# Weight gradients computed piece by piece inside attention forward, in a one-core backward kernel of a transformer block

## Chip, cores, metric

The kernel runs on one core of one Trainium2 chip. The metric is device microseconds (us) of one execution. Each time quoted is the median of the executions, with the lowest and highest. The times of the profile come from one profiled execution and lie within 0.3% of these.

## The reference

The kernel computes one transformer block (adaptive layer norm, attention, an MLP with a squared ReLU) and all gradients of it, in bf16, for 2048 tokens of width 512, 32 heads of 16, and an MLP width of 1792. Cut to what matters:

```python
def _fwd_reference(A_x, A_wqkv, A_wo, B_x, B_w1, B_b1, B_w2, B_b2, c, w_mod):
    mod = (silu(c) @ w_mod)                        # sa, ca, ga, sb, cb, gb
    h = layernorm(x) * (1 + ca) + sa
    x = x + ga * attention(h, A_wqkv, A_wo)        # softmax over 2048 keys, 32 heads
    h = layernorm(x) * (1 + cb) + sb
    x = x + gb * (relu(h @ B_w1 + B_b1) ** 2 @ B_w2 + B_b2)
    return x

def reference(...):
    out, vjp = jax.vjp(f, A_x, A_wqkv, A_wo, B_w1, B_b1, B_w2, B_b2, c, w_mod)
    return (out, *vjp(grad_out))                   # out_0, then nine gradients
```

Three of the nine gradients are in question here. They are sums over all 2048 tokens: out_3 (of `A_wo`, 512x512), out_4 (of `B_w1`, 512x1792) and out_6 (of `B_w2`, 1792x512).

## The kernel before

The five engines are called PE (TensorE), DVE (VectorE), ACT (ScalarE), POOL (GpSimd) and SP (SyncE, which only issues DMAs). P is 128, FC is 14 (1792 / 128), DC is 4 (512 / 128), QC is 4 (chunks of 512 queries).

Attention forward runs 512 "units". A unit is four heads, 512 queries and 128 keys: four matmuls for the scores, two exponentials of 128x1024 on ScalarE, four matmuls that multiply the values. When the 128 units of one query chunk are done, that chunk's "dense" work can start: output projection, layer norm, MLP forward, MLP backward, gradient of the attention output. It is a Python generator, and the loop takes one step of it per unit, so that its matmuls run while ScalarE takes exponentials. Chunks 0 to 2 are mixed in this way. Chunk 3 has nothing left to be mixed with and runs alone.

```python
with tc.manual_schedule(engines={PE.engine, ACT.engine}):
    for u in range(NF + 6):
        ...                              # fload, fscore(u): scores and exponentials
        if 2 <= u < NF + 2:
            fpv(u - 2)                   # exponentials times values
        if dense:
            if wait > 0:
                wait -= 1
            else:
                wait = next(dense[0], -1)     # one step of the dense chunk
                ...
```

The dense chunk, cut to the order of its parts and of its weight loads. `wA` and `wB` are one buffer each, so a load waits until the last reader of the former content is done:

```python
def dense_chunk(c, O_c, act):
    w1_nat = load_wA(False)
    w2_nat = load_wB(False)
    ...                                  # projection, layer norm, h2
    yield 10
    for fc in range(FC):                 # MLP forward with w1_nat
        ...
        yield 0
    w2T = load_wA(True)                  # four transposing DMAs
    yield 1
    for ti in range(4):                  # MLP output product with w2_nat: ~20 steps
        ...
    w1T = load_wB(True)
    for fc in range(FC):                 # MLP backward with w2T
        ...
    for ti in range(4):                  # gradient of h2 with w1T
        ...
    yield 8
    for ti in range(4):                  # gradient of the attention output, with woT
        ...
```

So before the change each weight load had other work in front of its first use: the transposed w2 had the whole output product.

After forward came a phase of its own for the three weight gradients. It loaded its operands again from DRAM, and built a padded transpose of `A_wqkv` (`wT_bld`) that the last phase needs:

```python
for key, src in (("gf", gf_st), ("O", o_st), ("da", da_st), ("h2", h2_st)):
    ...                                  # 2 MB each, back from DRAM
wT_bld = big.tile([P, 16, D], BF, name="wT_bld")
...                                      # 12 transposing loads, 96 small DMAs
for oc in range(DC):
    acc = psg.tile([P, 512], F32, name="aw", tag="aw")
    for t in range(TT):
        PE.matmul(acc[:], toks["O"][:, t, oc * P:(oc + 1) * P], toks["da"][:, t, :], ...)
    ...                                  # copy, DMA to out_3; then out_6 and out_4 alike
```

Attention backward follows (512 units of four heads, 128 queries and 512 keys, with four exponentials each; its transposes `dsT` are DMAs on the SP queue), and then a last phase.

Of the kernel before, what the change touches and what calls it, by code (L numbers as in the profile page):

```python
# [17 lines left out]
BF = dt.bfloat16  # L18
# [16 lines left out]
def kernel(  # L35
# [55 lines left out]
    da_st = dram.tile([P, TT, D], BF, name="da_st")  # L91
    h2_st = dram.tile([P, TT, D], BF, name="h2_st")
    gf_st = dram.tile([P, TT, D], BF, name="gf_st")
    q_st = dram.tile([P, TT, QPAD], BF, name="q_st")
    k_st = dram.tile([P, TT, QPAD], BF, name="k_st")
    stok_st = dram.tile([QC, P, 4 * FF], BF, name="stok_st")
    dztok_st = dram.tile([QC, P, 4 * FF], BF, name="dztok_st")
    wT_st = dram.tile([P, 16, D], BF, name="wT_st")
# [60 lines left out]
    for ic in range(DC):  # L159
        for t in range(3):  # L160
            src = wqkv_nat[:, ic, t * 512:(t + 1) * 512].rearrange("p (hg h d) -> p hg h d", hg=HG, h=4)
            dst = wpadT[:, ic, t].rearrange("p hg (h c) -> p hg h c", h=4)[:, :, :, 0:DH]
            POOL.tensor_copy(dst, src)

# [115 lines left out]
    with ExitStack() as ph:  # L280
# [43 lines left out]

        def dense_chunk(c, O_c, act):
            ts = slice(4 * c, 4 * c + 4)
            w1_nat = load_wA(False)
            w2_nat = load_wB(False)
# [6 lines left out]
            gf_c = cb.tile([P, 4, D], BF, name="gf_c", tag="hd")  # L335
            POOL.tensor_tensor(gf_c[:], g_c[:], gb_bc.unsqueeze(1).to_broadcast([P, 4, D]), ALU.mult)
            SP.dma_start(out=gf_st[:, ts, :], in_=gf_c[:])
# [33 lines left out]
            h2_c = cb.tile([P, 4, D], BF, name="h2_c", tag="hd")  # L371
            POOL.tensor_tensor(h2_c[:], xn2_c[:], cb1_bc.unsqueeze(1).to_broadcast([P, 4, D]), ALU.mult)
            POOL.tensor_tensor(h2_c[:], h2_c[:], sb_bc.unsqueeze(1).to_broadcast([P, 4, D]), ALU.add)
            SP.dma_start(out=h2_st[:, ts, :], in_=h2_c[:])
            yield 10
            rT = cb.tile([P, FC, 512], BF, name="rT", tag="rT")
            sT = cb.tile([P, FC, 512], BF, name="sT", tag="sT")

            def to_tokens(src, dst, f0, f1):
                tk = cb.tile([P, 16, P], BF, name="tk", tag="tk", bufs=2)  # L380
                SP.dma_start(out=tk[:, 0:4 * (f1 - f0), :], in_=flat(src[:, f0:f1, :]), transpose=True)
                SP.dma_start(out=dst[:, 512 * f0:512 * f1], in_=flat(tk[:, 0:4 * (f1 - f0), :]))

            for fc in range(FC):
# [9 lines left out]
                if fc % 4 == 3 or fc == FC - 1:  # L394
                    to_tokens(sT, stok_st[c], fc // 4 * 4, fc + 1)
# [3 lines left out]
            for ti in range(4):  # L399
                t = 4 * c + ti  # L400
                pf = mm()
                for fc in range(FC):
                    PE.matmul(pf[:], sT[:, fc, ti * P:(ti + 1) * P], w2_nat[:, fc, :], start=(fc == 0), stop=False)  # L403
                    if fc % 4 == 3:
                        yield 0
                PE.matmul(pf[:], ones_bf[0:1, 0:P], b2row[0:1, :], start=False, stop=True)
                gfprod = wk.tile([P, D], BF, name="gfprod", tag="ta")
                DVE.tensor_tensor(gfprod[:], pf[:], g_c[:, ti, :], ALU.mult)
                rowsum(0, gfprod[:], t)
                ftmp = wk.tile([P, D], BF, name="ftmp", tag="tb")  # L410
                DVE.tensor_tensor(ftmp[:], pf[:], gb_bc, ALU.mult)
                DVE.tensor_tensor(x1_c[:, ti, :], ftmp[:], x1_c[:, ti, :], ALU.add)
                yield 0
            SP.dma_start(out=out0_v[:, ts, :], in_=x1_c[:])
            w1T = load_wB(True)
            dzT = rT
            for fc in range(FC):
# [8 lines left out]
                if fc % 4 == 3 or fc == FC - 1:  # L426
                    to_tokens(dzT, dztok_st[c], fc // 4 * 4, fc + 1)
                yield 0
            yield 1
            dx1_c = cb.tile([P, 4, D], BF, name="dx1_c", tag="od")  # L430
            da_c = cb.tile([P, 4, D], BF, name="da_c", tag="hd")
            for ti in range(4):
                t = 4 * c + ti
                pdh = mm()
                for fc in range(FC):
                    PE.matmul(pdh[:], dzT[:, fc, ti * P:(ti + 1) * P], w1T[:, fc, :],
                              start=(fc == 0), stop=(fc == FC - 1))
                    if fc % 4 == 3:
                        yield 0
                xn2 = xn2_c[:, ti, :]  # L440
# [19 lines left out]
                DVE.tensor_tensor(da_c[:, ti, :], dx1_c[:, ti, :], ga_bc, ALU.mult)  # L460
                proda = wk.tile([P, D], BF, name="proda", tag="tc")
                DVE.tensor_tensor(proda[:], dx1_c[:, ti, :], a_c[:, ti, :], ALU.mult)
                rowsum(3, proda[:], t)
                yield 0
            SP.dma_start(out=dx1_st[:, ts, :], in_=dx1_c[:])
            daT = cb.tile([P, 4, DC, P], BF, name="daT", tag="T4")
            SP.dma_start(out=daT.rearrange("p t o q -> p (t o) q"), in_=flat(da_c), transpose=True)
            SP.dma_start(out=da_st[:, ts, :], in_=da_c[:])
            dOs_c = cb.tile([P, 4, D], BF, name="dOs_c", tag="od")
            dOp = flat(cb.tile([P, FC, 512], BF, name="dOp", tag="sT"))[:, 0:4 * HG * P]  # L470
            dOp = dOp.rearrange("p (t g c) -> p t g c", t=4, g=HG)
            POOL.memset(dOp, 0.0)
            yield 8
            for ti in range(4):
                t = 4 * c + ti
                pdo = mm()
                for oc in range(DC):
                    PE.matmul(pdo[:], daT[:, ti, oc, :], woT[:, oc, :], start=(oc == 0), stop=(oc == DC - 1))
                src = pdo.rearrange("q (g h d) -> q g h d", g=HG, h=4)
                dst = dOs_c[:, ti, :].rearrange("q (g h d) -> q g h d", g=HG, h=4)  # L480
                rb = r_inv[:, t, :].rearrange("q (g h) -> q g h", g=HG).unsqueeze(3).to_broadcast([P, HG, 4, DH])
                DVE.tensor_tensor(dst, src, rb, ALU.mult)
                POOL.tensor_copy(dOp[:, ti].rearrange("q g (h c) -> q g h c", h=4)[:, :, :, 0:DH], dst)
                prodo = wk.tile([P, D], BF, name="prodo", tag="tb")
                DVE.tensor_tensor(prodo[:], dOs_c[:, ti, :], O_c[:, ti, :], ALU.mult)
                delta = wk.tile([P, H], F32, name="delta", tag="delta")
                DVE.tensor_reduce(delta[:], prodo.rearrange("q (h d) -> q h d", d=DH), AX.X, ALU.add)
                auxdst = dOp[:, ti].rearrange("q g (h c) -> q (g h) c", h=4)[:, :, DH:DH + 1].rearrange("q h o -> q (h o)")
                DVE.tensor_scalar(auxdst, delta[:], -1.0, None, ALU.mult)
                if ti % 2 == 1:  # L490
                    dOT = cb.tile([P, 16, P], BF, name="dOT", tag="tk", bufs=2)
                    SP.dma_start(out=dOT[:], in_=dOp[:, ti - 1:ti + 1].rearrange("p t g c -> p (t g c)"), transpose=True)
                    q0 = c * 512 + (ti - 1) * P
                    for hg in range(HG):
                        SP.dma_start(out=dOtP[hg][:, q0:q0 + 2 * P].rearrange("p (t q) -> p t q", t=2),
                                     in_=dOT.rearrange("p (t g) q -> p g t q", t=2)[:, hg])
                yield 0
            SP.dma_start(out=dOs_st[:, ts, :], in_=dOs_c[:])
# [26 lines left out]
        def fpv(u):  # L525
# [13 lines left out]
            if kt == TT - 1:  # L539
                ostage = wk.tile([P, 512], F32, name="ostage", tag="ostage")  # L540
# [29 lines left out]
        with ExitStack() as ph2:  # L570
# [3 lines left out]
            with tc.manual_schedule(engines={PE.engine, ACT.engine}):  # L574
                for u in range(NF + 6):
# [6 lines left out]
                    if dense:  # L582
                        if wait > 0:
                            wait -= 1
                        else:
# [435 lines left out]
```

## Time and profile before

3380.86 us (3377.52 to 3382.63, four executions).

| stretch | from | to | us |
|---|---|---|---|
| preparation | 0 | 289 | 289 |
| attention forward, dense chunks 0 to 2 mixed in | 289 | 1279 | 990 |
| dense chunk 3 alone | 1279 | 1412 | 134 |
| weight-gradient phase | 1412 | 1617 | 205 |
| loads, then attention backward from its first exponential (1635) | 1617 | 3070 | 1453 |
| last phase | 3070 | 3386 | 316 |

The table of stretches of the kernel before comes first. Its columns are the stretch in us from the start, its length, the busy time of each engine with its number of instructions, the granted TensorE clock, the mean busy share of the DMA engines, and what they moved.

```profile
core 0: us, PE busy (x) PEld busy (x) DVE busy (x) ACT busy (x) POOL busy (x), PEclk, DMA share, GB/s
287.00:533.00 246.00, 225.56 (x1064) 42.26 (x1064) 5.54 (x8) 245.24 (x268) 8.98 (x9) 0.50 0.17 52
1040.00:1278.00 238.00, 207.21 (x1228) 56.21 (x1237) 89.52 (x172) 226.66 (x246) 47.09 (x45) 0.78 0.49 121
1278.00:1412.00 134.00, 73.03 (x271) 28.67 (x275) 78.22 (x159) 9.54 (x14) 39.24 (x38) 0.75 0.66 124
1412.00:1450.00 38.00, 1.18 (x3) 0.50 (x4) 1.28 (x2) 0.00 (x0) 6.93 (x1) 0.51 0.68 223
1450.00:1617.00 167.00, 114.63 (x536) 53.97 (x540) 10.32 (x17) 10.30 (x18) 1.20 (x1) 0.84 0.42 152
```

In forward ScalarE is full: 245.24 of 246 us with attention alone, 226.66 of 238 with a dense chunk mixed in. In the two weight-gradient rows ScalarE does almost nothing (0 and 10.30 us), and TensorE works for 116 of 205 us. So these 205 us are serial, and the change wants to put their matmuls under ScalarE's exponentials.

That there is room is shown by one unit of forward with a dense step, from the time line of TensorE of the kernel before (start, us, engine, line, operation, output and inputs, count):

```profile
648.18 1.02 PE L420 MATMUL pm<-gfT,wA 128*128 128x512 bf16 x4
649.13 0.39 PE L521 MATMUL psST<-qt_sb,kt_sb 32*128 32x512 bf16 x4
649.46 0.40 PE L537 MATMUL oacc<-ET,vaug 128*32 128x512 bf16 x4
```

A unit lasts 1.92 us for ScalarE, and TensorE needs 0.39 + 0.40 us for attention and 1.02 us for four dense matmuls of 128x512.

The group of the forward exponentials on the page of the kernel before says how much ScalarE waited: its busy time, the mean of one in ns, then its idle time just before these instructions and what ended most of it.

```profile
L523 ACT ACTIVATE ET<-psST 128x1024 bf16<-128x1024 f32 x1024 | 945.5, 1311 | 34.7 <-PE psST L521 34.5
```

### The profile page before, as it was taken

The numbers are of one execution on the slowest core, as the hardware profiler recorded it, in microseconds if no ns is written. First come the engines' busy times: TensorE is split into PE (matmuls) and PEld (weight loads), VectorE is DVE, ScalarE is ACT, GpSimd is POOL, SyncE is SP. The second block draws the span as 40 slices with busy tenths as digits, with TensorE's granted clock in tenths as the row PEclk, the third lists the DMA queues.
The fourth block names the chain that finished last, engine by engine and source line by source line (L and its number), as shares of the span: only waits on it lengthen the run. The fifth ranks groups of instructions, "written<-read, shape, count | busy, mean of one in ns | idle before, by whom it ended". The sixth has DMA issues, their size and how long they took to land.

```text
span 3386.2 us, 47396 instructions
## 1 busy us (share of the span) xinstructions
PE 2663.9 (79%) x17485; PEld 788.3 (23%) x17549; DVE 1932.1 (57%) x2770; ACT 2157.3 (64%) x3474; POOL 372.3 (11%) x345
## 2 busy tenths in 40 slices
PE   2778998888888885348697889898898978885746
PEld 1232111221221222114122222222222222222312
DVE  8852002332343344400587878788887878884772
ACT  0006999999999992000586878787787868784202
POOL 3000001121121132300110010101010101010000
PEclk7986555975975976778788878888878889897867
DMA  3124001661662654763999999999999999997113
GB/s 128 55 107 150 29 29 47 136 173 52 138 166 57 137 155 100 167 211 115 219 200 213 199 211 197 207 205 204 208 198 209 198 215 201 201 201 182 63 62 94
DMA packets 1388742, 511.31 MB, mean 151 GB/s; under 512 B 1321939, under 2 KB 1359575, under 8 KB 1386205
## 3 DMA queue, kind: packets, MB, share of 16 engines
q1 hardware_dynamic: 1368782, 502.51, 70.8%
q10 hardware_dynamic: 19728, 5.77, 0.8%
q8 instruction: 138, 2.26, 0.3%
q14 instruction: 94, 0.77, 0.1%
HBM read 112.29 MB, written 74.08 MB: 55 GB/s over the span
## 4 chain that ended last, share of the span: by engine, by line
PE 36%; DMA 21%; ACT 18%; DVE 12%; issue 6%; SPq 3%; ACTq 2%; POOL 0%; DVEq 0%; POOLq 0%
DMA dsT<-dS_u 16%; ACT ET L523 14%; PE psS_u L724 7%; PE dqacc L776 5%; ACT E_u L726 4%; PE accVK L761 3%; PE ppad L266 3%; PE accVK L752 2%; PE psST L521 2%; DVE dS_u L738 2%; PE psS_x L724 2%; PE pm L387 2%; ACTq L636 1%; PE pm L420 1%; PE pm L403 1%
## 5 line engine op out<-in xcount | busy, mean ns | idle before, releaser
L738 DVE TENSOR_TENSOR dS_u<-psD_u,E_u 128x1024 bf16<-128x1024 f32 x1024 | 1189.4, 1218 | 248.5 <-PE psD_u L736 166.5
L726 ACT ACTIVATE E_u<-psS_u 128x512 bf16<-128x512 f32 x1536 | 866.3, 633 | 307.2 <-PE psD_u L736 274.0
L523 ACT ACTIVATE ET<-psST 128x1024 bf16<-128x1024 f32 x1024 | 945.5, 1311 | 34.7 <-PE psST L521 34.5
L724 PE MATMUL psS_u<-ik,iq 32*128 32x512 bf16 x1536 | 517.2, 434 | 27.0 <-DVE KS_tok L677 19.1
L521 PE MATMUL psST<-qt_sb,kt_sb 32*128 32x512 bf16 x2048 | 464.6, 507 | 85.2 <-ACT ET L523 37.7
L736 PE MATMUL psD_u<-iv,ido 32*128 32x512 bf16 x2048 | 448.4, 432 | 18.9 <-DVE dS_u L738 11.4
L776 PE MATMUL dqacc<-dsT,KS_tok 128*32 128x512 bf16 x2048 | 212.7, 503 | 161.0 <-DMA dsT<-dS_u 149.2
L726 ACT ACTIVATE E_u<-psS_x 128x512 bf16<-128x512 f32 x512 | 333.9, 652 | 2.2 <-PE psD_u L736 1.7
L537 PE MATMUL oacc<-ET,vaug 128*32 128x512 bf16 x2048 | 270.4, 517 | 0.6 <-ACT ET L523 0.6
L541 DVE COPY ostage<-oacc 128x512 f32<-128x512 f32 x32 | 22.0, 688 | 373.6 <-PE oacc L537 373.6
L761 PE MATMUL accVK<-E_u,dOs_tok 128*16 128x512 bf16 x2048 | 226.3, 432 | 0.0
L724 PE MATMUL psS_x<-ik,iq 32*128 32x512 bf16 x512 | 210.6, 411 | 0.6
L521 PEld LDWEIGHTS <-kt_sb 32*128 32x128 bf16 x2048 | 91.4, 96 | 461.7 <-issue 456.8
L724 PEld LDWEIGHTS <-iq 32*128 32x128 bf16 x2048 | 99.1, 93 | 378.6 <-issue 378.0
L736 PEld LDWEIGHTS <-ido 32*128 32x128 bf16 x2048 | 124.8, 93 | 228.4 <-issue 203.7
L791 POOL TENSOR_TENSOR dQacc<-dQacc,dqtmp 128x512 f32<-128x512 f32 x64 | 81.1, 1268 | 843.0 <-ACT dqtmp L786 843.0
L641 ACT ACTIVATE wblk<-aw 128x512 bf16<-128x512 f32 x9 | 5.4, 597 | 229.4 <-PE aw L648 125.2
L752 PE MATMUL accVK<-dS_u,qz_12652 128*32 128x512 bf16 x1024 | 113.1, 430 | 6.8 <-ACT vkb L764 5.8
L752 PE MATMUL accVK<-dS_u,qz_12651 128*32 128x512 bf16 x1024 | 112.0, 427 | 7.0 <-ACT vkb L764 6.1
L266 PE MATMUL ppad<-xn1T,wpadT 128*128 128x512 bf16 x376 | 98.7, 408 | 21.8 <-DVE stagep L269 16.2
L850 ACT ACTIVATE dqkv_tok<-ptq 128x64 bf16<-128x64 bf16 x128 | 28.6, 224 | 119.8 <-PE ptq L844 119.8
L776 PEld LDWEIGHTS <-KS_tok 128*32 128x32 bf16 x2048 | 52.1, 105 | 221.2 <-issue 179.0
(1021 smaller groups left out, 2496.9 us busy)
## 6 DMA issues: line engine op xcount, KB each, us to landing
kt_sb<-KtP SPq DMA_DIRECT2D x32, 512.0 KB, 3.7
dsT<-dS_u SPq DMA_TRANSPOSE x512, 5.1
wA<-in_B_w_dram SPq DMA_DIRECT2D x4, 1792.0 KB, 8.8
wB<-in_B_w_dram SPq DMA_DIRECT2D x4, 1792.0 KB, 7.7
stok_st<-tk SPq DMA_DIRECT2D x12, 512.0 KB, 3.0
dztok_st<-tk SPq DMA_DIRECT2D x12, 512.0 KB, 4.0
QtP<-stagep SPq DMA_DIRECT2D x8, 512.0 KB, 2.8
KtP<-stagep SPq DMA_DIRECT2D x8, 512.0 KB, 2.9
```

The source lines that it names most:

```text
L266: PE.matmul(pp[:], wpadT[:, ic, which, hg, :], h1T[:, ic, qc * 512:(qc + 1) * 512], start=(ic == 0), stop=(ic == DC - 1))
L521: PE.matmul(ps[:, hi, :], kt_sb[r:r + 32, kt * P:(kt + 1) * P], qt_sb[r:r + 32, :], start=True, stop=True, tile_position=(r, 0))
L523: ACT.activation(ET[:, 2 * pair:2 * pair + 2, :], ps[:], AF.Exp, scale=SCALE)
L537: PE.matmul(oacc[32 * hq:32 * hq + 32, :], lhsT, ET[:, hq, :], start=(kt == 0), stop=(kt == TT - 1), tile_position=(0, 32 * hq), skip_grou ...
L724: PE.matmul(psS[:], st["q"][r:r + 32, qt * P:(qt + 1) * P], st["k"][r:r + 32, kc * 512:kc * 512 + 512], start=True, stop=True, tile_positi ...
L726: ACT.activation(bst[u][0][:, hq, :], psS[:], AF.Exp, scale=SCALE)
L736: PE.matmul(psD[:, hi, :], st["do"][r:r + 32, qt * P:(qt + 1) * P], st["v"][r:r + 32, kc * 512:kc * 512 + 512], start=True, stop=True, til ...
L738: DVE.tensor_tensor(dS_u[:, 2 * pair:2 * pair + 2, :], psD[:], E_u[:, 2 * pair:2 * pair + 2, :], ALU.mult)
L752: PE.matmul(cur["vk"][32 * hq:32 * hq + 32, :], hst[hg]["qz"][:, qt, hq, :], bst[u][1][:, hq, :], start=(qt == 0), stop=False, tile_positi ...
L761: PE.matmul(acc[32 * hq:32 * hq + DH, :], dOs_tok[:, qt, (hg * 4 + hq) * DH:(hg * 4 + hq + 1) * DH], E_u[:, hq, :], start=False, stop=(qt ...
L776: PE.matmul(acc[32 * hq:32 * hq + 32, :], KS_tok[:, kc * 4 + kt, h * DH:h * DH + 32], tT[:, :, hq * 4 + kt, :], start=(kt == 0), stop=(kt ...
L791: POOL.tensor_tensor(dst2, dst, tmp[:], ALU.add)
```

## The change

Intent: take the weight-gradient phase out. Each chunk computes its share of the three gradients at once, while its operands are still in SBUF, as 34 "pieces". A piece is four matmuls (128 tokens each, 512 columns, 256 in four of the pieces), a VectorE copy into one of three buffers `dwp`, and a DMA into a partial sum in DRAM: chunk 0 writes it, chunks 1 and 2 add to it in the DMA (`accum_op`), chunk 3 loads it, adds it to its own result and writes the output. At most one piece runs per unit, and only in units without a dense step. To have the operands of the pieces early, the MLP output product is placed behind the MLP backward. The padded transpose of `A_wqkv` is written row-wise during preparation and read by 16 transposing DMAs at the start of attention backward.

```diff
-    da_st = dram.tile([P, TT, D], BF, name="da_st")
-    ...                                  # h2_st, gf_st, stok_st, dztok_st, wT_st
+    dw_st = dram.tile([DC + FC + 16, P, 512], F32, name="dw_st")
+    wpad_st = dram.tile([D, 16 * P], BF, name="wpad_st")
 ...
+        def dw_piece(c, i, dst, ops, w):
+            if c == QC - 1:
+                part = wk.tile([P, 512], F32, name="dwp", tag="dwp", bufs=3)
+                SP.dma_start(out=part[:, 0:w], in_=dw_st[i][:, 0:w])
+            acc = mm()
+            for ti in range(4):
+                PE.matmul(acc[:, 0:w], ops[ti][0], ops[ti][1], start=(ti == 0), stop=(ti == 3))
+            if c == QC - 1:
+                res = wk.tile([P, 512], BF, name="dwr", tag="ta")
+                DVE.tensor_tensor(res[:, 0:w], acc[:, 0:w], part[:, 0:w], ALU.add)
+                SP.dma_start(out=dst, in_=res[:, 0:w])
+            else:
+                part = wk.tile([P, 512], F32, name="dwp", tag="dwp", bufs=3)
+                DVE.tensor_copy(part[:, 0:w], acc[:, 0:w])
+                if c == 0:
+                    POOL.dma_start(out=dw_st[i][:, 0:w], in_=part[:, 0:w])
+                else:
+                    POOL.dma_start(out=dw_st[i][:, 0:w], in_=part[:, 0:w], accum_op=ALU.add)
 ...
         def dense_chunk(c, O_c, act):
             w1_nat = load_wA(False)
-            w2_nat = load_wB(False)
+            w1T = load_wB(True)
 ...                                       # MLP forward; its pieces are queued by later(dw_piece, ...)
             w2T = load_wA(True)
             yield 1
-            for ti in range(4):           # MLP output product
-                ...
-            w1T = load_wB(True)
             ...                           # MLP backward with w2T, then gradient of h2 with w1T
+            def mlp_out():
+                w2_nat = load_wB(False)
+                yield 1
+                ...                       # the output product, as before
+            if act:                       # chunk 3
+                yield 0
+                yield from attn_grad()
+                yield from mlp_out()
+            else:
+                yield from mlp_out()
+                yield from attn_grad()
 ...                                       # in the loop over units:
+                    if pend and pend[0][0] <= u and not open_group[0] and not stepped:
+                        _, f, args = pend.pop(0)
+                        f(*args)
 ...
-    with ExitStack() as ph:               # the weight-gradient phase and wT_bld: removed
-        ...
 ...
         load_head(0)
+        for j in range(16):
+            SP.dma_start(out=wT_pad[:, j, :], in_=wpad_st[:, j * P:(j + 1) * P], transpose=True)
```

## The prediction

> **What bounds the kernel now.** One core, 3381.5 us. The table of stretches shows: preparation to 287 us; attention forward with dense chunks 0 to 2 mixed in, 287 to 1278; dense chunk 3 alone, to about 1412; the weight-gradient phase to 1617; attention backward to 3073; the rest to 3386. In attention forward ScalarE is the limit: 227 of 238 us busy in 1040:1278; a unit takes 1.92 us. TensorE has room: a timeline at 646 us shows a unit as 0.39 us of scores, 0.40 of PV and 1.02 of four dense matmuls, with ScalarE at 30.0 of 30.0 us in 616:646. The weight-gradient phase is serial: 115 us of TensorE in 1450:1617, before it about 40 us of reloads and building wT.
>
> **Removed.** The weight-gradient phase: -205 us, all on the chain of waits.
>
> **Added in attention forward.** 34 pieces per chunk: four matmuls, a 0.69 us VectorE copy, a GpSimd DMA adding 256 KB into DRAM. About 3 run in the dense chunk's waits; 31 run one per unit after its end. The matmuls cost what a dense step costs, so I expect them hidden under ScalarE, with the granted clock near 1.0 (the Trainium skill, "TensorE: Matmul & The Clock Gate", Part 1: activity releases the half clock; the trace agrees: 0.50 in 740:786 with attention only, 0.92 to 1.00 with dense steps). An accumulating DMA must come from GpSimd (the skill, "DMA: Bandwidth & Descriptors", SWDGE vs HWDGE vs iDMA); this trace has none. With three buffers it may take about 5 us before the engines wait. I allow +15 us, uncertain.
>
> **Moved: the product behind the backward.** Two weight loads lose their cover. Transposed w2 must land two units (3.9 us) after its buffer is free; its four transposes take 1.5 to 3.3 us each to issue and 5.5 us to land: about 15 us, so TensorE stalls 10 to 12 us and ScalarE about 10. Plain w2 (8 us to land): ScalarE about 3. Three chunks: +39 us. ScalarE gaps of about 4 us at 734, 985, 1235 may go: -9. Attention forward in sum: +45 us (+25 to +80).
>
> **Chunk 3 alone (134 us now)** gains 34 pieces, each with a partial-sum load, an add and an output DMA: 0.95 us TensorE, 0.7 VectorE, partly in gaps (7 us each for w2 and OT, 6 for daT). I expect 150 to 165 us: +22.
>
> **Start of backward.** About 20 us of loads stay. Sixteen transposed wT loads on the same queue ahead of dsT: +5. One 2 MB load less in the last phase: -5.
>
> **Sum.** 3381 - 205 + 45 + 22 = about 3245 us. Range 3190 to 3310. Faster by over 2%: 0.90; within 2%: 0.08; slower: 0.02.
>
> **What would show it.**
> - No serial weight-gradient stretch; backward's first exponential near 1500 us instead of 1635.
> - Attention forward 1015 to 1070 us instead of 991; per chunk one ScalarE gap of 8 to 12 us while TensorE waits for the DMA into wA, one of 2 to 5 for wB.
> - The 31-piece stretches: unit 1.9 to 2.2 us, clock near 1.0. A unit of 2.5 us, with VectorE copies waiting for the accumulate DMA, would mean that the DMA limits.
> - The chunk-3 stretch 150 to 165 us.
>
> **What would make it wrong.** An accumulating DMA of 8 us or more (a unit 0.8 us longer in 93 units: +75 us); chunk-3 pieces serialized behind one in-order DMA queue (+40); wT transposes holding up dsT (+20); or w2 loads hidden better than I think (-35).

## The result, and the profile after

The changed kernel took 3342.85 us (3337.01 to 3347.24, four executions) against 3380.86: a ratio of 0.9888 (95% interval 0.987 to 0.9905). A ratio is the mean time of one kernel's runs over that of the other's of the same rounds, so it isn't quite the ratio of the medians. The prediction was 3245 us with a range of 3190 to 3310; the measured time lies 33 us above that range.

To say where the time went, forward is cut by its units: the k-th pair of exponentials in the trace is unit k. A dense chunk occupies 92 units (135 to 227, 263 to 355, 391 to 483). The 32 units after it (for chunk 2 the 29 units to the end of forward) are called the late stretch here; there the 31 remaining pieces run, one per unit. "Chunk 3 and on" goes from forward's last exponential to backward's first.

| us in the trace | before | after | difference |
|---|---|---|---|
| preparation | 289.0 | 291.3 | +2 |
| three dense parts | 177.9 / 176.6 / 176.7 | 192.6 / 191.9 / 189.6 | +43 |
| three late stretches | 65.2 / 64.3 / 59.6 | 75.1 / 87.7 / 86.8 | +60 |
| chunk 3 and on (before: and the weight gradients) | 356.5 | 192.4 | -164 |
| backward, first to last exponential | 1434.8 | 1460.4 | +26 |
| last phase | 316.1 | 308.9 | -7 |
| span | 3386.2 | 3345.0 | -41 |

(The rest of forward, attention alone, changed by about 1 us. One late stretch is known only roughly: wt_in_j and tail_bufs, two of the runs below whose edits don't touch forward, have 94.9 and 97.3 us for chunk 1 where after has 87.7, and 1097.0 and 1098.3 us for the whole of forward where after has 1092.1.) Of the 205 us of the phase that went, four fifths came back elsewhere. The table of stretches of the kernel after, with the same columns:

```profile
core 0: us, PE busy (x) PEld busy (x) DVE busy (x) ACT busy (x) POOL busy (x), PEclk, DMA share, GB/s
289.50:541.00 251.50, 228.94 (x1084) 43.09 (x1077) 8.78 (x16) 249.04 (x272) 8.96 (x9) 0.50 0.18 49
1022.00:1090.00 68.00, 42.95 (x256) 12.98 (x253) 17.79 (x29) 40.60 (x43) 28.32 (x29) 0.82 1.14 185
1107.00:1384.00 277.00, 219.19 (x1352) 64.41 (x1348) 107.90 (x198) 228.00 (x245) 72.39 (x76) 0.85 0.59 110
1384.00:1562.00 178.00, 102.81 (x423) 42.26 (x420) 94.74 (x195) 8.69 (x13) 41.44 (x43) 0.78 0.68 150
1562.00:1576.00 14.00, 4.99 (x10) 0.69 (x9) 2.71 (x4) 1.57 (x2) 4.70 (x3) 0.62 0.74 248
```

The row 1022:1090 lies in a late stretch: ScalarE worked only 40.60 of 68 us, and TensorE 42.95. Neither is full, so something else sets the pace. Chunk 3 alone took 178 us instead of 134, with 102.81 us of TensorE instead of 73.03.

From the page of after: the queue that holds the new DMAs (packets, MB, share of the DMA engines), the forward exponentials, and the new DMAs in its list of issues (count, KB of one, median us from issue to landing):

```profile
q0 software_dynamic: 12384, 25.17, 4.2%
...
L580 ACT ACTIVATE ET<-psST 128x1024 bf16<-128x1024 f32 x1024 | 948.9, 1260 | 133.6 <-PE psST L578 133.1
...
dw_st<-dwp POOLq DMA_DIRECT2D x90, 256.0 KB, 4.8
```

The 25.17 MB are the 102 pieces of chunks 0 to 2. ScalarE's wait for scores rose from 34.5 to 133.1 us: nearly 100 us of forward, as the table says. The longest waits of after in the stretch 1022:1090 (engine, buffer and line, what was waited for: us in all, times, longest):

```profile
DVE dwp L347 <- DMA dw_st<-dwp: 31.2, 9, 6.4
POOL dw_st L351 <- DVE dwp L347: 30.4, 16, 4.7
ACT ET L580 <- PE psST L578: 27.3, 11, 6.8
PE pm L340 <- DVE dwp L347: 24.4, 10, 6.0
```

This is read from the top down: the VectorE copy waits for the accumulating DMA that still reads its buffer (31.2 us), TensorE's next piece waits for the copy (24.4 us), since `pm` has one bank in this phase, and ScalarE waits for the scores that stand behind the piece on TensorE (27.3 us). GpSimd waits for the copy in turn (30.4 us), so it is mostly the landing that is waited for. Mostly, since once in this stretch three of the DMAs stand in GpSimd's queue behind another product (`gf_c`), which itself waits 5.0 us; the runs plain, pool_order and best1 come back to this.

In the dense part, the time line of ScalarE of after at the load of the transposed w2 (in brackets the idle time before and what ended it):

```profile
628.78 1.94 ACT L580 ACTIVATE ET<-psST 128x1024 bf16<-128x1024 f32 x2 [7.84 <-PE psST L578]
```

And the time line of TensorE of after at the loads of both forms of w2:

```profile
620.38 0.39 PE L437 MATMUL pm<-gfT,wA 128*128 128x512 bf16 x1 [1.43 <-DMA wA<-in_B_w_dram]
623.72 0.61 PE L437 MATMUL pm<-gfT,wA 128*128 128x512 bf16 x1 [2.94 <-DMA wA<-in_B_w_dram]
625.79 0.61 PE L437 MATMUL pm<-gfT,wA 128*128 128x512 bf16 x1 [1.47 <-DMA wA<-in_B_w_dram]
627.53 0.61 PE L437 MATMUL pm<-gfT,wA 128*128 128x512 bf16 x1 [1.13 <-DMA wA<-in_B_w_dram]
...
695.42 1.89 PE L499 MATMUL pm<-wB,sT 128*128 128x512 bf16 x4 [3.86 <-DMA wB<-in_B_w_dram]
```

TensorE waits for each of the four transposes in turn, and ScalarE stands for 7.84 us. In the three chunks these two gaps of ScalarE were 7.8, 11.0 and 8.6 us for `wA` and 4.4, 3.4 and 3.4 us for `wB`: 39 us, as predicted.

In chunk 3 alone, the time line of VectorE of after:

```profile
1490.93 0.69 DVE L343 TENSOR_TENSOR dwr<-pm,dwp 128x512 bf16<-128x512 f32 x1 [3.79 <-DMA out_dram<-dwr]
1501.48 0.69 DVE L343 TENSOR_TENSOR dwr<-pm,dwp 128x512 bf16<-128x512 f32 x1 [9.73 <-DMA out_dram<-dwr]
```

The result buffer `dwr` has two copies, shared with three other tiles, and waits up to 9.73 us for an output DMA. At the start of backward, the SP queue of after:

```profile
1571.54 0.42 SPq L707 DMA_DIRECT2D ido<-dOtP  x1
1572.87 28.82 SPq L803 DMA_TRANSPOSE wT_pad<-wpad_st  x16
1601.79 4.15 SPq L750 DMA_TRANSPOSE dsT<-dS_u  x2
```

In before the same queue went from `ido` to `dsT` at once:

```profile
1639.86 0.43 SPq L701 DMA_DIRECT2D ido<-dOtP  x1
1640.43 5.70 SPq L744 DMA_TRANSPOSE dsT<-dS_u  x1
```

In after the 16 transposes hold the queue for 28.82 us, and backward's own `dsT` stands behind them. Backward's first 64 exponentials (16 units) took 70.0 us instead of 47.4.

### The profile page after: what moved, and what is told of

It reads as the page before. It is cut to its first block, busy times and chain, and to the rows that moved or that the text cites. A ratio compares the mean times of both kernels' runs of the same rounds, so it can differ in the third digit from the quotient of the medians.

```text
span 3345.0 us, 47765 instructions
## 1 busy us (share of the span) xinstructions
PE 2615.0 (78%) x17549; PEld 775.1 (23%) x17549; DVE 2004.4 (60%) x2889; ACT 2151.9 (64%) x3457; POOL 442.9 (13%) x458
## 3 DMA queue, kind: packets, MB, share of 16 engines
q0 software_dynamic: 12384, 25.17, 4.2%
## 4 chain that ended last, share of the span: by engine, by line
PE 34%; DMA 24%; ACT 16%; DVE 12%; issue 8%; SPq 4%; POOL 1%; DVEq 0%; POOLq 0%; ACTq 0%
DMA dsT<-dS_u 16%; ACT ET L580 11%; PE psS_u L730 6%; ACT E_u L732 5%; PE dqacc L782 5%; PE accVK L767 3%; PE ppad L270 3%; PE accVK L758 2%; PE psST L578 2%; DVE dS_u L744 2%; DMA dw_st<-dwp 2%; PE psS_x L730 2%; PE pm L417 2%; PE pm L437 1%; PE pm L499 1%
## 5 line engine op out<-in xcount | busy, mean ns | idle before, releaser
L580 ACT ACTIVATE ET<-psST 128x1024 bf16<-128x1024 f32 x1024 | 948.9, 1260 | 133.6 <-PE psST L578 133.1
L578 PE MATMUL psST<-qt_sb,kt_sb 32*128 32x512 bf16 x2048 | 399.4, 477 | 65.8 <-ACT ET L580 30.6
L594 PE MATMUL oacc<-ET,vaug 128*32 128x512 bf16 x2048 | 253.2, 485 | 1.3 <-DVE ostage L598 1.3
L578 PEld LDWEIGHTS <-kt_sb 32*128 32x128 bf16 x2048 | 83.3, 94 | 403.5 <-issue 392.7
L347 DVE COPY dwp<-pm 128x512 f32<-128x512 f32 (+1 forms) x102 | 67.2, 659 | 176.8 <-PE pm L340 98.2
L340 PE MATMUL pm<-tk,h_c 128*128 128x512 bf16 (+1 forms) x256 | 71.4, 409 | 63.7 <-DVE dwp L347 52.7
(1022 smaller groups left out, 2563.9 us busy)
```

The source lines that it names most:

```text
L578: PE.matmul(ps[:, hi, :], kt_sb[r:r + 32, kt * P:(kt + 1) * P], qt_sb[r:r + 32, :], start=True, stop=True, tile_position=(r, 0))
L580: ACT.activation(ET[:, 2 * pair:2 * pair + 2, :], ps[:], AF.Exp, scale=SCALE)
L594: PE.matmul(oacc[32 * hq:32 * hq + 32, :], lhsT, ET[:, hq, :], start=(kt == 0), stop=(kt == TT - 1), tile_position=(0, 32 * hq), skip_grou ...
```

## The experiments

My theory for the late stretches, the largest loss: the pace is the return of the three buffers `dwp`, that is, the landing time of the accumulating DMA. Rivals: the extra matmuls and copies crowd out the scores; the cost is any write, not the addition; or the DMA is slow only because the 14 transposes of the next chunk's w1 crowd it. For the dense parts: uncovered weight loads. For chunk 3: two buffers in series. For the start of backward: the transposes on the SP queue. Each run is an edit of the kernel after, except where two are combined. All give correct results but nodma and plain, which are wrong. The four calls of timed kernels each shared their own executions of before (3380.26, 3382.96, 3384.61 and 3383.94 us).

The late stretches of all kernels that bear on the pieces, in us, with the median landing time of the pieces' DMAs in 1020:1110, where read:

| kernel | chunk 0 | chunk 1 | chunk 2 | landing |
|---|---|---|---|---|
| before | 65.2 | 64.3 | 59.6 | |
| after | 75.1 | 87.7 | 86.8 | 6.1 |
| nodma | 75.5 | 64.2 | 57.9 | |
| plain | 75.2 | 74.4 | 70.1 | 3.6 |
| bf16_three | 73.1 | 77.2 | 73.7 | 4.1 |
| bf16_six | 70.1 | 72.8 | 68.6 | 4.5 |
| plain_weights | 70.5 | 93.9 | 88.5 | 5.4 |
| best2 | 64.8 | 67.7 | 63.1 | 3.3 |

### nodma: chunks 1 and 2 don't write their pieces

```diff
                 if c == 0:
                     POOL.dma_start(out=dw_st[i][:, 0:w], in_=part[:, 0:w])
-                else:
-                    POOL.dma_start(out=dw_st[i][:, 0:w], in_=part[:, 0:w], accum_op=ALU.add)
```

> Chunks 1 and 2 keep their piece matmuls and VectorE copies but send nothing to DRAM (three weight gradients wrong on purpose). Base is the changed kernel: its 31-piece stretches take 75.1, 87.7 and 86.8 us (65.2, 64.3 and 59.6 before the change). Theory A, the DMA that empties the three buffers sets the pace: chunks 1 and 2 fall to 62 to 68 us, chunk 0 stays at 75, the kernel is 40 to 50 us faster than the changed one (about 3298). Rival B, four more matmuls per unit do not fit beside attention: 85 us or more stay, the time stays near 3343. Rival C, the late transposes and the dOp work block the queues: it stays above 78.

Measured: 3283.68 us (3282.38 to 3288.82), ratio 0.9717 (0.97 to 0.9733). The late stretches of chunks 1 and 2 fell to 64.2 and 57.9 us, which is before's 64.3 and 59.6; chunk 0, which still writes, stayed at 75.5. From the table of stretches of nodma, one in the middle of the pieces (same columns):

```profile
1013.00:1077.00 64.00, 56.20 (x362) 18.26 (x360) 22.90 (x38) 58.70 (x65) 11.23 (x9) 0.92 0.61 133
```

ScalarE works 58.70 of 64 us, and TensorE has more to do than in after (56.20) without harm. So the matmuls and copies of the pieces are free, and the rival of crowded-out scores falls. All of the loss hangs on the DMA, be it by its landing or by its place in GpSimd's queue; the gain over after, 59 us, is more than the 40 to 50 expected.

### plain: chunks 1 and 2 write without adding

```diff
-                    POOL.dma_start(out=dw_st[i][:, 0:w], in_=part[:, 0:w], accum_op=ALU.add)
+                    POOL.dma_start(out=dw_st[i][:, 0:w], in_=part[:, 0:w])
```

> The DMA of chunks 1 and 2 overwrites instead of accumulating (wrong on purpose), everything else equal. If the read-add-write itself is what is slow, both stretches fall to the 75 us of chunk 0, which writes plainly: about 25 us off 3343, so 3318. If only the number of buffers against a crowded DMA queue counts, they stay at 82 to 88 and the time within 8 us of 3343.

Measured: 3308.99 us (3306.01 to 3310.52), ratio 0.9785 (0.9771 to 0.98). The late stretches were 74.4 and 70.1 us. So writing at all costs 10 and 12 us a chunk over nodma (chunk 0, which in after only writes, agrees: 75.1 against 65.2 before), and the addition another 13 and 17. The pieces' DMAs in 1020:1110, of after first and then of plain (the counted issues with least, median and greatest ns of the issuing, and their landing times):

```profile
L351 POOL DMA_DIRECT2D dw_st<-dwp x28: 856/862/1513, 1019.2 to 1100.3; - x28
DMA to landing us min/median/max: 3.2/6.1/11.3
```

```profile
L351 POOL DMA_DIRECT2D dw_st<-dwp x26: 539/539/580, 1020.6 to 1082.4; - x26
DMA to landing us min/median/max: 2.0/3.6/5.7
```

The arithmetic fits: three buffers at one piece per 1.92 us give each 5.8 us for its round. The copy takes 0.69 us and the handover to GpSimd about 0.3 us (an estimate from the time line), so a DMA has to land within some 4.8 us. A median of 6.1 doesn't, and at 3.6, with the greatest at 5.7, most do.

The landing isn't all, though. The time lines of GpSimd and of VectorE of plain, in the late stretch of chunk 1:

```profile
1035.56 4.05 POOL L366 TENSOR_TENSOR gf_c<-g_c,modbc 128x2048 bf16<-128x2048 bf16 x1 [5.32 <-DMA g_c<-in_grad_out_dram]
1039.55 1.65 POOL L351 DMA_DIRECT2D dw_st<-dwp  x3
...
1042.44 0.69 DVE L347 COPY dwp<-pm 128x512 f32<-128x512 f32 x1 [6.88 <-DMA dw_st<-dwp]
```

The product `gf_c`, which belongs to the next chunk, waits 5.32 us for its load and then takes 4.05 us. Three writes stand behind it in GpSimd's queue, so all three buffers are full, VectorE waits 6.88 us, and ScalarE has a gap of 7.3 us. In chunk 2 the gap at this place is 8.5 us. So most of the 10 and 12 us that plain writes still cost is time in the queue and not in landing.

### bf16_six and bf16_three: half the bytes, with six buffers and with three

```diff
-    dw_st = dram.tile([DC + FC + 16, P, 512], F32, name="dw_st")
+    dw_st = dram.tile([DC + FC + 16, P, 512], BF, name="dw_st")
 ...
-                part = wk.tile([P, 512], F32, name="dwp", tag="dwp", bufs=3)
+                part = wk.tile([P, 512], BF, name="dwp", tag="dwp", bufs=6)    # 3 in bf16_three
```

(A small tile `prows` that shared these buffers moved to another tag.) Six buffers in f32 don't fit: a build with them stops, since the last SBUF pool of this phase asks for 80 KB per partition and 74.3 are left. So bf16_six changes bytes and buffers at once, and bf16_three was run to part them.

> Partial sums in bfloat16: half the bytes per DMA, and six buffers in the same space (the result is rounded twice more). Theory A: with twice the buffers the waits for the accumulating DMA (34.7 and 26.0 us) nearly go: stretches of 65 to 72 us instead of 75.1, 87.7, 86.8, so 35 to 50 us off 3343. Rival B (TensorE) or C (late transposes, dOp): 80 us or more stay for chunks 1 and 2.

> bf16_six with three buffers instead of six: half the bytes, the same count as in the change. The late stretches are 75.1, 87.7, 86.8 us with the change and 70.1, 72.8, 68.6 with bf16_six. If the landing time against three buffers is what counts and halving the bytes shortens it to about 4 us, most of the gain stays: 74 to 80 us. If the count of buffers is the point, they are 82 us or more.

Measured: bf16_six 3306.47 us (3305.03 to 3311.99), ratio 0.9778 (0.9762 to 0.9795); bf16_three 3307.86 us (3305.46 to 3314.75), ratio 0.9777 (0.9763 to 0.9792). The late stretches of chunks 1 and 2 fell by 15 and 18 us in bf16_six, and by 10.5 and 13 in bf16_three. So half the bytes bring most of it, by landing sooner (4.1 us), and three more buffers another 3 to 5 us a chunk there. (In the whole time the two runs are equal within 1.4 us: in the profiled executions preparation, which the edit doesn't touch, and chunk 3 are 5.5 and 3.3 us longer in bf16_six.) In bf16_six chunks 1 and 2 remain 8 to 9 us above before, and each has one ScalarE gap of that size (7.9 and 8.5 us) where the product `gf_c` stands at the head of GpSimd's queue. Rounding the partial sums to bf16 is a loss of accuracy that the change did not have.

### plain_weights: fewer transposes next to the pieces

The transposed w1 and w2 are written to DRAM in chunk 0, and chunks 1 to 3 load them plainly.

```diff
-            w1T = load_wB(True)
+            w1T = load_wB(True, c)       # c > 0: SP.dma_start(out=w[:], in_=w1T_st[:])
 ...
-            w2T = load_wA(True)
+            w2T = load_wA(True, c)       # c > 0: SP.dma_start(out=w[:], in_=w2T_st[:])
```

> The transposed w1 and w2 are transposed once, kept in DRAM and loaded plainly for chunks 1 to 3, so fewer transposing DMAs run beside the pieces. If the accumulating DMA lands late (6 us and up to 11.8, against 4.6 us in a quiet stretch) because it queues behind transposes: the landing falls to about 5 us, the late stretches of chunks 0 to 2 by 5 to 10 us each, and the wA gaps of chunks 1 and 2 from 11.0 and 8.6 to 3 to 5 us: 25 to 40 us off 3343. If crowding does not matter: only the wA gaps shrink, about 10 us off.

Measured: 3334.6 us (3333.94 to 3337.51), ratio 0.9855 (0.984 to 0.9869). The late stretches of chunks 1 and 2 did not fall (93.9 and 88.5), and the landing stayed above 5 us in the median (5.4 in 1020:1110). The gain of 8 us comes from the dense parts (186.1 and 183.6 instead of 191.9 and 189.6), where ScalarE's gap for `wA` fell from 11.0 and 8.6 us to 5.0 and 4.6. So crowding by the weight transposes isn't confirmed as the cause of slow landings.

### cover and bf16_cover: waiting units in front of the weight loads' first uses

```diff
             w2T = load_wA(True)
-            yield 1
+            yield 7
 ...
                 w2_nat = load_wB(False)
-                yield 1
+                yield 4
```

A waiting unit has no dense step, so a piece can run in it. bf16_cover adds the edit of bf16_six.

> Eight units instead of two between the last product that needs w1 and the first that needs the transposed w2, and five instead of two for the plain w2; pieces run in these waits. Theory: the dense stretches lost 15, 15 and 13 us to the two uncovered loads. Then the ScalarE gaps of 8 to 11 us (wA) and 3.4 to 4.4 us (wB) go, and, as fewer pieces are left for the crowded stretch, attention forward falls from 1092 us by 35 to 50: about 3300. Rival: the dense stretch is long because of something else that the reorder brought; the gaps only move and the time stays above 3330.

> cover on top of bf16_six. cover alone lost 11 us, because pieces that run in the waits met accumulating DMAs of up to 17.7 us with three buffers; with half the bytes and six buffers the waits should carry them. Dense stretches about 177 us instead of 187 to 192, late stretches 75 to 80 with fewer pieces: attention forward about 1033 us instead of 1049, 3306 becomes about 3288. If the gain of best1 came from elsewhere the dense stretches stay at 187 or more.

Measured: cover 3354.34 us (3347.98 to 3363.08), ratio 0.9922 (0.9903 to 0.9942): 11 us slower than after, a miss. The dense parts came to 184.6, 194.4 and 201.4 us. Its trace shows four ScalarE gaps of 13 to 17 us. One (15.0 us) lies inside the dense part of chunk 2, where pieces had moved into the waiting units: beside a weight load and two transposing DMAs, an accumulating DMA took up to 17.7 us to land, and three buffers don't last that long. The other three (13.4, 16.5 and 17.0 us) lie in the late stretches, where the product `gf_c` waits 11.3 to 11.8 us at the head of GpSimd's queue. bf16_cover shows that the idea was right for the dense parts: 3278.17 us (3275.44 to 3283.15), ratio 0.9688 (0.9673 to 0.9702), with dense parts of 177.6, 177.8 and 177.2 us against before's 177.9, 176.6 and 176.7. So nearly all of the +43 us of the dense parts is lost cover of weight loads (bf16_six alone takes 5 us off them). But of the 36 us that cover takes off the dense parts of bf16_six, 19 come back in the late stretches, which rise from 70.1, 72.8 and 68.6 to 77.2, 79.1 and 74.6 us, each with one ScalarE gap of 14 us. Forward as a whole falls by 17 us; the rest of the 28 us between the two runs lies in stretches that the edit doesn't touch.

### old_order: pieces as in after, the MLP output product where it was

```diff
             w1_nat = load_wA(False)
-            w1T = load_wB(True)
+            w2_nat = load_wB(False)
 ...
             w2T = load_wA(True)
             yield 1
+            yield from mlp_out()
+            w1T = load_wB(True)
 ...
-            if act:
-                ...
-            else:
-                yield from mlp_out()
-                yield from attn_grad()
+            yield 8
+            yield from attn_grad()
```

> The pieces stay, the MLP output product goes back ahead of the MLP backward, with its weight loads where they were before the change. Theory: the placing behind the backward costs 35 to 45 us in the dense stretches of attention forward. Then the ScalarE gaps for wA and wB vanish; the gaps of about 4 us near the end of each dense chunk return only if they came from the dOp work; the time falls by 20 to 45 us, to about 3310. Rival: the order is neutral and the pieces alone lengthen the dense part: the time stays within 10 us of 3343.

Measured: 3312.45 us (3309.99 to 3317.33), ratio 0.9794 (0.9779 to 0.9808), so the move alone costs 30 us in the change as made. The dense parts are 178.5, 176.9 and 177.9, the late stretches of chunks 1 and 2 stay long (86.0 and 85.0), and chunk 3 and on grows from 192.4 to 211.1. At the place of the 7.84 us gap, ScalarE of old_order runs through 22 exponentials without a break:

```profile
611.89 20.33 ACT L575 ACTIVATE ET<-psST 128x1024 bf16<-128x1024 f32 x22
```

The move loses 41 us in the dense parts and 8 in the late stretches, and gains 19 in chunk 3.

### tail_bufs and bf16_tail: the buffers of chunk 3

```diff
-                res = wk.tile([P, 512], BF, name="dwr", tag="ta")
+                res = ework.tile([P, 512], BF, name="dwr", tag="ET")
```

The `ET` buffers are idle in chunk 3. bf16_tail adds the edit of bf16_six, which gives the loaded partial sums six buffers.

> The sum of each chunk-3 piece goes into one of four exp tiles that are free by then, instead of the two small buffers shared with the layer-norm gradient. Theory: VectorE lost 22.9 us waiting for the output DMA to free a buffer, 13.5 of it in two waits at 1487 and 1492. Then the stretch from the last exponential of attention forward to the first of backward falls from 192 us to 170 to 180, the time to about 3328. Rival: TensorE or the loads of the partial sums set it; it stays at 188 or more.

> tail_bufs on top of bf16_six. The stretch from forward's last exponential to backward's first is 192 us with the change, 185 with tail_bufs, 194 with bf16_six, and 167 in best1, which has both. If two waits stand in series, for the output buffer and for the loaded partial sum, freeing both gives 165 to 172 us. If the gain of best1 came from cover or from the wT loads it stays at 180 or more.

Measured: tail_bufs 3339.44 us (3332.74 to 3350.42), ratio 0.9875 (0.9852 to 0.9898); chunk 3 and on 184.9 us instead of 192.4, where 170 to 180 were expected: a miss. bf16_six, without this edit, left that stretch at 193.6. Both together (bf16_tail): 167.0 us, and 3275.23 us in all (3272.82 to 3280.48), ratio 0.9679 (0.9663 to 0.9696). The waits of VectorE in chunk 3, of after and then of tail_bufs, say why one alone does little:

```profile
DVE dwr L343 <- DMA out_dram<-dwr: 22.9, 8, 9.7
DVE dwr L343 <- DMA dwp<-dw_st: 12.2, 5, 8.2
```

```profile
DVE dwr L343 <- DMA dwp<-dw_st: 13.6, 10, 3.6
```

With the output buffer free, the add waits for the loaded partial sum more often (10 times instead of 5). The two waits take turns, and only the pair of edits takes them both away: 25 us. (bf16_tail also halves the bytes of each loaded sum; no run says how much of the 25 us is bytes and how much is buffers.)

### wt_in_j: the transposes out of the start of backward

```diff
-        for j in range(16):
-            SP.dma_start(out=wT_pad[:, j, :], in_=wpad_st[:, j * P:(j + 1) * P], transpose=True)
 ...                                       # in the last phase, per head group hg:
+                for j in (hg, 8 + hg):
+                    SP.dma_start(out=wT_pad[:, j, :], in_=wpad_st[:, j * P:(j + 1) * P], transpose=True)
```

> The sixteen transposed loads of wT move from the start of attention backward to the head loop of the phase after it, two per head group. Theory: they held the queue for 28.8 us ahead of the first dsT; then the first 16 units of backward fall from 70.0 to about 47 us and the last phase grows by at most 6 us: 15 to 24 us faster, about 3322. Rival: the loads of q, k, v at the start are slow for another reason; the 70 us stay.

Measured: 3330.8 us (3329.75 to 3342.65), ratio 0.9859 (0.984 to 0.9878), 12 us below after, where 15 to 24 were expected. Backward's first 16 units took 52.7 us instead of 70.0 (before: 47.4); the last phase took 315.4 instead of 308.9. The SP queue of wt_in_j at the start of backward has no transposes of `wT_pad` left:

```profile
1579.78 0.43 SPq L705 DMA_DIRECT2D ido<-dOtP  x1
1595.09 30.53 SPq L748 DMA_TRANSPOSE dsT<-dS_u  x11
```

In after the first `dsT` was issued 30.3 us after `ido` (1571.54 to 1601.79); here it is 15.3 us. So the transposes are the cause of 17 of the 22.6 us lost there. The remaining 5 us are open. In wt_in_j TensorE waits 9.2 us for the load of `ido` after backward has begun, which the trace of before doesn't show there; no run tests whether that is the cause.

### pool_order, best1 and best2: GpSimd's queue, and all edits together

best1 joins cover, wt_in_j, tail_bufs and bf16_six. pool_order lets GpSimd's first work of the next dense chunk be issued only after the last accumulating DMA of the chunk before:

```diff
-            POOL.tensor_tensor(gf_c[:], g_c[:], gb_bc.unsqueeze(1).to_broadcast([P, 4, D]), ALU.mult)
+            with tc.issue_after(last_acc[0].ins) if last_acc[0] is not None else ExitStack():
+                POOL.tensor_tensor(gf_c[:], g_c[:], gb_bc.unsqueeze(1).to_broadcast([P, 4, D]), ALU.mult)
```

best2 is best1 with plain_weights and pool_order.

> One thing changed: the GpSimd product for the next chunk's gf is queued behind the last accumulating DMA of the chunk before. Theory C (the GpSimd queue is in order; that product waits at its head for the next chunk's gradient load while three ready accumulating DMAs stand behind it): the late stretches of chunks 0 and 1 lose 5 to 10 us each, about 12 to 18 us off 3343, so 3328. Theory A alone (landing time and three buffers): under 5 us off.

> cover, wt_in_j, tail_bufs and bf16_six together. If the four causes are separate their gains add, about 40 + 20 + 14 + 40 us, less some overlap between cover and bf16_six, which relieve the same crowded stretch: 3343 - 100, about 3240, which is what had been predicted for the change. If they hide each other it stays above 3270.

> best1 with pool_order and plain_weights added. In best1 one gap of 14.4 us per chunk is left at the head of the GpSimd queue (764, 1029, 1294 us). If theory C names it, the three gaps go: 3242 - 35 to 45, about 3200. If they move to the next wait in line, 3225 or more.

Measured: pool_order alone 3345.35 us (3338.02 to 3345.7), ratio 0.988 (0.9865 to 0.9894): nothing gained over after, where theory C expected 12 to 18 us. In the traces of plain_weights and old_order, too, the product waits 0.4 us or less for its load in the late stretches. In all three runs the late stretches of chunks 1 and 2 stay at 84.8 to 93.9 us. So with accumulating DMAs of f32 it gains nothing to free the head of the queue alone, while with the lighter writes of plain and bf16_six most of what is left sits there.

best1: 3241.85 us (3241.13 to 3242.19), ratio 0.9583 (0.9569 to 0.9597). The expected number was met, but partly by luck: it was the sum of single gains of 40, 20, 14 and 40 us, less some overlap, and the single gains came out as -11, 12, 3 and 36 us, 40 in all against 101 together. The causes aren't separate; the edits need each other.

best2: 3211.64 us (3207.36 to 3212.96), ratio 0.9485 (0.947 to 0.9501), which beats before by 5.2% and after by 3.9%; it is 30 us below best1, where 35 to 45 were expected.

In best1 the late stretches were still 77.3, 79.2 and 74.6 us, with one ScalarE gap of 14 us per chunk. The time line of GpSimd of best1 shows where it comes from:

```profile
1002.09 0.88 POOL L351 DMA_DIRECT2D dw_st<-dwp  x1 [10.08 <-DVE dwp L347]
1014.34 4.04 POOL L366 TENSOR_TENSOR gf_c<-g_c,modbc 128x2048 bf16<-128x2048 bf16 x1 [11.37 <-DMA g_c<-in_grad_out_dram]
1018.33 2.65 POOL L351 DMA_DIRECT2D dw_st<-dwp  x3
...
1021.09 3.14 POOL L524 MEMSET dOp<- 128x2048 bf16 x1
```

And the time line of VectorE of best1 just after:

```profile
1024.26 0.86 DVE L538 TENSOR_SCALAR dOp<-delta 128x32 bf16<-128x32 f32 x2 [13.31 <-POOL dOp L524]
```

The product `gf_c` at the head of GpSimd's queue waits 11.37 us for a load. Behind it stand accumulating DMAs, but the six buffers don't run out: VectorE has filled only five since the last DMA before the wait. What stands behind it as well is the clearing of `dOp`; VectorE comes to a small instruction on `dOp` that waits 13.31 us for it, and the copy of the next piece comes only after that one. So the wait passes from one queue to the next, and ScalarE's gap is 14.4 us. The Trainium skill, "TensorE: Matmul & The Clock Gate", Part 1, states that the queue of each of GpSimd's cores is strictly first in, first out; this trace agrees, with the 11.37 us. In best2 2.5 to 3.2 us of the gap are left, and forward takes 995.0 us against before's 989.8. Its row in the table of stretches of best2 (same columns):

```profile
287.00:1282.00 995.00, 883.43 (x5233) 244.61 (x5275) 344.01 (x628) 952.58 (x1034) 217.06 (x246) 0.79 0.44 101
```

ScalarE is busy for 952.58 of 995 us. So with the obstacles of forward out of the way, the weight gradients cost it 5 us. best2 differs from best1 by two edits, plain_weights and pool_order, and no run parts them; in the trace of plain_weights the product's wait is already gone (0.3, 0.0 and 0.0 us in the three late stretches), so both may act on the same gap.

## Why the prediction was wrong

Step by step, as the prediction's sum had it (differences to before, from the traces):

| term | predicted | measured | shown by |
|---|---|---|---|
| weight-gradient phase gone | -205 | -205 | stretches |
| pieces in forward | +15 | +60 | nodma, plain, bf16_three |
| weight loads of the moved product | +39 - 9 = +30 | +43 | bf16_cover, old_order |
| chunk 3 alone | +22 | +44 | bf16_tail |
| start of backward | +5 | +22 | wt_in_j |
| preparation, last phase | -5 | -5 | stretches |
| sum | -138 | -41 | |

(Measured: chunk 3 is 178 - 134 us. The start of backward is +25.6 us from first to last exponential and about -3.5 us in front of the first one. Preparation is +2, the last phase -7.)

1. **"I allow +15 us, uncertain"** for the pieces is the step that failed most: they cost 60 us, and these 45 us are nearly half of the 97 us by which the sum was off. The mechanism was in the text: "With three buffers it may take about 5 us before the engines wait". The working above gives nearly the same limit (4.8 us, an estimate). What was wrong is the size of the landing: an accumulating DMA took 6.1 us where the pieces run, not under 5. Against "A unit of 2.5 us, with VectorE copies waiting for the accumulate DMA": the late stretch of chunk 1 is 87.7 us for 32 units and that of chunk 2 86.8 us for 29, that is 2.7 and 3.0 us per unit, with exactly this wait. What the prediction did not have is the rest of GpSimd's queue: with plain writes, which land after 3.6 us, 10 us per chunk stay, most of it in the one gap of 7 to 8 us behind the product `gf_c`.

2. **The weight loads.** The gaps came as predicted (39 us); the dense parts lost 43, and where the last 4 us sit is not shown. "ScalarE gaps of about 4 us ... may go: -9" is the other part of the 13 us by which this term is off. Those gaps lie in the late stretches of before (4.1, 3.7 and 3.5 us), and the late stretches gained nothing, so this saving is not to be seen; whether it is hidden in the +60 is not shown.

3. **"I expect 150 to 165 us: +22"** for chunk 3. It was 178 us. The matmul time came nearly as costed (+30 us of TensorE for 34 pieces, 0.88 each, against 0.95), but I had put it partly into gaps, and did not see that the result tile has two shared buffers, nor that the loaded sum has three. With both widened, chunk 3 and on falls by 25 us to 167.0: that would make the stretch 153 us, inside the range.

4. **"Sixteen transposed wT loads on the same queue ahead of dsT: +5."** They held the queue for 28.82 us and cost 17 of the 22 us. The trace of before had the price: its 56 transposes of w1, 512x128 each like these, took 1.26 us in the median to issue, which gives 20 us for 16 (an estimate). The prediction named this among its risks ("wT transposes holding up dsT (+20)") and gave it the wrong place, in the risks and not in the sum.

5. **What was right.** The serial phase went whole; backward's first exponential lay at 1576 us (I said "near 1500"; the forward and chunk-3 misses account for the difference). The Trainium skill, "DMA: Bandwidth & Descriptors", section "SWDGE vs HWDGE vs iDMA", says that an accumulating DMA must come from GpSimd; the trace agrees in so far as the 68 accumulating DMAs (and the 34 plain writes of chunk 0) are all issued there, on the queue that the profile's page calls software_dynamic, and no run tried another. The expectation that four full matmuls per unit bring the clock up held in nodma, 0.92 in the middle of the pieces. In after it was 0.82 in 1022:1090, where TensorE was busy for 42.95 of 68 us. (In 740:786 TensorE was busy for 42.23 of 46 us at 0.50; see the last section.)

In each failed term it was the size that was off, and all four in the same direction, so the errors added up, and the range was too narrow for that. My reading, which no run tests as such, is that each part was costed as if the others left its buffers and queues alone.

## What to carry to other kernels

When work is moved under a busy engine, its engine time is the easy part: the matmuls of 68 pieces cost nothing here, and their DMAs, through three staging buffers, cost about 25 us per chunk in chunks 1 and 2. So work out the time that a buffer's round may take (buffers times the interval, less the copy) and compare it with the slowest landing under load, not with the median of a quiet stretch. Look as well at what else stands in the queue that issues the DMAs. Where a wait is removed and nothing moves, look for the second wait in series before giving the idea up: cover alone lost 11 us, and on top of half the bytes and six buffers it won 28 (17 of them in forward).

## What the Trainium skill lacked or had wrong

- "DMA: Bandwidth & Descriptors", section "Anatomy of one DMA": the fit of 2.0 us plus bytes / 436e3 gives an estimate of 2.6 us for 256 KB. In these runs a plain write of 256 KB from GpSimd landed after 3.6 us (2.0 to 5.7). For an accumulating DMA to DRAM the page has no figure: 4.6 us in a quiet stretch (three of them, 4.1 to 5.8), a median of 6.1 us (3.2 to 11.3) when the pieces run, and up to 17.7 us next to a weight load and transposes.
- The same page has no time for issuing a transposing DMA of this size on Trainium2 (only a cycle count for small tiles of earlier generations): 16 of 512x128 in bf16 from DRAM held the SP queue for 28.8 us, 1.8 us each; the 56 of w1 in before, of the same size, took 1.26 us in the median.
- "TensorE: Matmul & The Clock Gate", Part 1, says that the clock follows how busy TensorE has been. Here that isn't enough. In attention alone TensorE was busy 225.56 of 246 us before the change, and 228.94 of 251.50 after it, at a granted clock of 0.50 both times; those matmuls use 32 rows or 32 columns of the array. With matmuls of 128x128 mixed in the clock was 1.00 at 49.74 busy of 55 us (after, 698:753). The page makes such an exception for transposes only (Part 4); no run says what in the attention matmuls keeps the clock down.
- No page says what a waiting instruction at the head of GpSimd's queue costs the work behind it: in best1 it waits 11.37 us, and by way of VectorE's queue ScalarE gets a gap of 14.4 us.
